# Attention visits of four key tiles where they hold a part, and norms dealt out per visit, in a fused attention and feed-forward kernel

## The chip, the cores and the metric

One core of one Trainium2 chip. The metric is the device time of one execution in microseconds (us), the median of several runs. The kernel before: 424.99 us, median of three runs from 424.94 to 425.61. The core's engines run side by side, each through its own queue in program order: TensorE (PE, matrix products), VectorE (DVE), ScalarE (ACT, functions such as exp), GpSimd (POOL), and SyncE (SP), which here only issues DMAs. Products are written to PSUM, eight banks per partition, and have to be read out of it by ACT or DVE before a bank is used again.

## The reference

Eight batches of twelve heads, 448 rows, head size 64. Each query and key row is divided by its norm, the scores are divided by tau = 0.1, softmax over the keys, times the values. The heads side by side are the 3584 x 768 input of a feed-forward layer with 2048 hidden columns:

```python
q_n = q / (norm(q, axis=-1) + 1e-06)
k_n = k / (norm(k, axis=-1) + 1e-06)
attn = softmax(q_n @ k_n.T / tau)          # per batch and head
x = (attn @ v) laid out as (3584, 768)
h = x @ moe_w_in                           # 768 -> 2048
out = maximum(0.01 * h, h) @ moe_w_out     # 2048 -> 768, float32
```

## The kernel before

**Feed-forward.** The 3584 tokens are cut into eight chunks, alternately 384 and 512 tokens wide. A chunk has 16 calls of `first` (six 128x128 matmuls each, then a leaky ReLU on ACT into `hT`) and then, for each 128 tokens, two calls of `second` (16 matmuls with 384 columns, then a copy on DVE and the DMA of the output rows by SP). A chunk can begin when the attention of its batches is in `xT`. These calls are the "feed", and together they are most of PE's work.

**Attention, its opening.** The first batches go through an opening that is laid out by hand (loops over `s`, `opened`). The change leaves this part alone, apart from the number of buffers of two pools.

**Attention, its stream.** The other 18 blocks of four heads (j = 6 to 23) are ten `GROUPS` of one or two, cut into 18 `UNITS` of two head pairs each. A unit has seven key tiles of 64 keys. One tile (`quad_tiles`) is eight small matmuls (64 rows, 32 columns, 448 queries) that run side by side in the array and fill two PSUM banks; ACT takes the exponential of both banks at once (128x896) into a `pe` buffer. The 126 tiles follow each other in `stream`, and are taken in "visits". When all tiles of a group are done, its "parts" follow, one in each of the next visits: the sums of the exponentials (`e` is None; then `group_logs` and `group_inverse` on ACT), and the values for `e` = 0 and, for groups of two, `e` = 1 (then `group_scale` on DVE, into `xT`). A part is 56 small matmuls (`group_products`) into one pair of banks. The parts of the last group come after the stream.

**A visit** (L795 to L849) issues, in this order: `normalise(s)` of a slot; `prepare()`; one tile; the part, if there is one; the other two tiles; then feed calls, with `roots(s + 1)` ahead of the last of them. Where a group of one is scaled (`alone`), `prepare()` stands behind the part.

**The norms.** A slot `s` is the queries (even) or keys (odd) of one unit. Its way: `load_qk` (two DMAs, SP) four slots ahead; `squares` (POOL); `sums` (DVE, 128x896 to 128x14); `roots` (ACT, three small operations); `normalise` (DVE, reciprocal and product, into a `qn` buffer); `transposes` (DVE, and for odd slots six DMAs on SP that bring both halves of the unit to `qkT`). `hold` is a small copy on POOL that reads `qn`, so that POOL's work behind it starts no earlier. In visit n with slot s the kernel normalises and transposes s, loads s + 4, squares s + 2, sums s + 1, and takes the roots of s + 1. `preps` gives each slot a visit of its own, three to four visits ahead of its unit.

**The planner.** `level` is the largest even share of feed per visit that the chunks' times of readiness (`at`) allow; `share` takes off the part's own cost (`side`); calls are taken from `held` while they fit. The plan is made when the program is built, so that the number of calls in each visit is fixed.

**Banks.** `banks(count)` gives the pair, or the single bank, whose last use lies furthest back, over all eight banks during the stream.

**Pools.** `qn` has three buffers, `pe` 25, `qkT` six, `ld` (raw loads) four, `hT` one.

Of the kernel before, what the change touches and what calls it, by code (L numbers as in the profile page):

```python
# [16 lines left out]
def kernel(  # L17
# [20 lines left out]
    NSLOT = B * NPAIR  # L38
# [5 lines left out]
    ATTEND = 5500  # L44
    BLOCK = 1800
    NEWQ = 2 * NQ
    PER = 3
    assert REM == 64 and D == 64

    ctx.enter_context(tc.manual_schedule())  # L50
# [2 lines left out]
    vbp = ctx.enter_context(tc.tile_pool(name="vb", bufs=3))  # L53
    sqp = ctx.enter_context(tc.tile_pool(name="sq", bufs=3))
    smp = ctx.enter_context(tc.tile_pool(name="small", bufs=3))
    qnp = ctx.enter_context(tc.tile_pool(name="qn", bufs=3))
    ttp = ctx.enter_context(tc.tile_pool(name="tt", bufs=2))
    qtp = ctx.enter_context(tc.tile_pool(name="qt", bufs=6))
    pep = ctx.enter_context(tc.tile_pool(name="pe", bufs=25))
    vqp = ctx.enter_context(tc.tile_pool(name="vq", bufs=2))  # L60
    rbp = ctx.enter_context(tc.tile_pool(name="rb", bufs=2))
    xtp = ctx.enter_context(tc.tile_pool(name="xt", bufs=2))
# [57 lines left out]
    OLD = 2 * NEWQ  # L120
# [7 lines left out]
    def load_qk(s, engs=(nc.sync, nc.sync)):  # L128
        if s >= NSLOT:
            return  # L130
        whole = ldp.tile([128, 14 * D], F32, name="qk_h")
        if s >= OLD:
            u, which = divmod(s - OLD, 2)
            for w, pair in enumerate(UNITS[u][1]):
                b, h0 = pair // NPAIR, 2 * (pair % NPAIR)
                nc.sync.dma_start(
                    out=whole[64 * w : 64 * w + 64],
                    in_=(q, k)[which][b, h0 : h0 + 2].rearrange("h (p t) d -> (h p) (t d)", t=14),
                )
            raw[s] = whole  # L140
            return
        b, h0 = s // NPAIR, 2 * (s % NPAIR)
        q_h, k_h = halves(whole)
        engs[0].dma_start(out=q_h[:, :, 0:3], in_=main(q, b, h0, 2))
        engs[1].dma_start(out=k_h, in_=main(k, b, h0, 2))
        for i, (x, eng) in enumerate(zip((q, k), engs)):
            eng.dma_start(
                out=q_h[64 * i : 64 * i + 64, :, 3],
                in_=x[b, h0 : h0 + 2, MAIN:S].rearrange("h p d -> p h d"),
            )  # L150
        raw[s] = (q_h, k_h)
# [20 lines left out]
    GROUPS = [(6,), (7, 8), (9, 10), (11,)] + [(j, j + 1) for j in range(12, 24, 2)]  # L172
# [22 lines left out]
    def squares(s, engs=(gp, gp)):  # L195
        if s >= NSLOT:
            return
        sq = sqp.tile([128, 14 * D], F32, name="sq")
        if s >= OLD:
            sqs[s] = sq  # L200
            gp.tensor_tensor(sq, raw[s], raw[s], op=ALU.mult)  # L201
            return
        sqs[s] = halves(sq)
        for x, y, eng in zip(raw[s], sqs[s], engs):
            if eng is nc.scalar:
                nc.scalar.activation(y, x, func=AF.Square)
            else:
                eng.tensor_tensor(y, x, x, op=ALU.mult)  # L208

    def sums(s, parts=(0, 1)):  # L210
        if s >= NSLOT:
            return
        if s not in ss:
            ss[s] = smp.tile([128, 14], F32, name="ss")
        if s >= OLD:
            nc.vector.tensor_reduce(  # L216
                ss[s], sqs[s].rearrange("p (t d) -> p t d", d=D), axis=AX.X, op=ALU.add
            )
            return
        for i in parts:  # L220
            o = ss[s][:, 0:8] if i == 0 else ss[s][:, 8:14]
            nc.vector.tensor_reduce(
                o.rearrange("p (h t) -> p h t", h=2), sqs[s][i], axis=AX.X, op=ALU.add
            )
# [8 lines left out]
    qn = {}  # L233

    def normalise(s):
        if s >= NSLOT:
            return
        r = smp.tile([128, 14], F32, name="r")
        nc.vector.reciprocal(r, ss[s])  # L239
        if s >= OLD:  # L240


            qn[s] = qnp.tile([128, 7, D, 2], BF16, name="qn")
            t, n = ("(m e)", "(e m)")[s % 2], 2
            nc.vector.tensor_tensor(  # L245
                qn[s].rearrange("p m d e -> p m e d"),
                raw[s].rearrange(f"p ({t[1:-1]} d) -> p m e d", e=n, d=D),
                r.rearrange(f"p {t} -> p m e", e=n).unsqueeze(3).to_broadcast([128, 7, 2, D]),
                op=ALU.mult,
            )  # L250
            return
        qn[s] = qnp.tile([128, 7, 2, D], BF16, name="qn")
        for x, lo, hi, r0 in ((raw[s][0], 0, 4, 0), (raw[s][1], 4, 7, 8)):
            nt = hi - lo
            nc.vector.tensor_tensor(  # L255
                qn[s][:, lo:hi],
                x.rearrange("p h t d -> p t h d"),
                r[:, r0 : r0 + 2 * nt].rearrange("p (h t) -> p t h", h=2)
                .unsqueeze(3).to_broadcast([128, nt, 2, D]),
                op=ALU.mult,  # L260
            )
# [129 lines left out]
    def quad_tiles(which):  # L391

        tiles = []
        for u, i in which:
            sc = banks(2)
            tiles.append(sc)
            for strip in range(4):
                x = qkT[UNITS[u][1][strip // 2]]
                c0 = S + 64 * i + 32 * (strip % 2)
                for a in range(2):  # L400
                    rows = slice(64 * a, 64 * a + 64)
                    nc.tensor.matmul(  # L402
                        out=sc[32 * strip : 32 * strip + 32, a, :S], lhsT=x[rows, c0 : c0 + 32],
                        rhs=x[rows, 0:S], start=True, stop=True,
                    )
        for (u, i), sc in zip(which, tiles):
            pq[u, i] = pe_tile()
            nc.scalar.activation(out=pq[u, i], in_=sc[:, :, :S], func=AF.Exp, scale=inv_tau)  # L408
# [169 lines left out]
    def hold(x):  # L578
        seen = smp.tile([128, 1], F32, name="seen")
        gp.tensor_copy(out=seen, in_=x)  # L580
# [183 lines left out]


    stream = [(u, i) for u in range(len(UNITS)) for i in range(7)]
    visits = [stream[n : n + PER] for n in range(0, len(stream), PER)]
    visit_of = {ui: n for n, tiles in enumerate(visits) for ui in tiles}
    parts, ready, last = {}, {}, 0
    for g, js in enumerate(GROUPS):  # L770
        last = max(last, max(visit_of[u, 6] for u, (gg, _) in enumerate(UNITS) if gg == g))
        for e in (None, 0, 1)[: 1 + len(js)]:
            last += 1
            parts[last] = (g, e)
        ready.update({j: last + 1 for j in js})
    at = {1: 0}
    for c in range(2, B):
        at[c] = ready[NQ * c + NQ - 1]
    preps, last = {}, -1
    for s in range(OLD + 3, NSLOT):  # L780
        last = max(last + 1, visit_of[(s - OLD) // 2, 0] - 4 + (s - OLD) % 2)
        preps[last] = s

    def weight(kind, cost):
        return cost * 0.7 if kind else cost
# [8 lines left out]
    held = [(False, g) for g in queue]  # L794
    fed = 0  # L795
    for n, tiles in enumerate(visits):
        s = preps.get(n, NSLOT)
        g, e = parts.get(n, (None, None))
        alone = g is not None and e is not None and len(GROUPS[g]) == 1

        def prepare():
            if s < NSLOT:
                transposes(s)
                load_qk(s + 4)
                hold(qn[s][:, 6, 0, 0:1])
                squares(s + 2)
                sums(s + 1)

        normalise(s)
        if not alone:  # L810
            prepare()
        quad_tiles(tiles[:1])
        if n == 0:
            attend(NEWQ - 1)
        if g is not None:
            po = group_products(g, e)
            if e is None:
                group_logs(g, po)
            else:
                group_scale(g, e, po)  # L820
        if alone:
            prepare()
        quad_tiles(tiles[1:])
        if g is not None and e is None:
            group_inverse(g)
        for u, i in tiles:
            if i == 6 and u and UNITS[u][0] != UNITS[u - 1][0]:
                load_vq(UNITS[u][0])
        for c in marked:
            if at[c] == n:  # L830
                held += marked[c]
        level = min(
            (sum(loads[c] for c in loads if at[c] <= x) - fed + sum(side[n : x + 1])) / (x - n + 1)
            for x in range(n, len(visits))
        )
        share = (level - side[n]) / (4 if n == len(visits) - 1 else 1)
        now, done = [], 0
        while held:
            w = weight(held[0][0], held[0][1][0])
            if now and done + w / 2 > share:  # L840
                break
            now.append(held.pop(0)[1][1])
            done += w
        fed += done
        for fn in now[:-1]:
            fn()
        roots(s + 1)
        for fn in now[-1:]:
            fn()  # L849
    g = len(GROUPS) - 1  # L850
    group_logs(g, group_products(g, None))
# [46 lines left out]
```

## Time and profile before

| | |
|---|---|
| median of three runs | 424.99 us |
| profiled execution: time, span | 425.26 us, 423.5 us |
| PE busy | 413.2 us, 98% |
| ACT busy | 267.8 us, 63% |
| DVE busy | 212.0 us, 50% |
| POOL busy | 114.7 us, 27% |
| DMA | 53.82 MB, 127 GB/s mean |
| `second`, PE matmuls (L502) | 151.4 us, 896 of 326 ns |
| `first`, PE matmuls (L474) | 151.1 us, 768 of 353 ns |
| key tiles in the stream (L402) | 38.9 us, 1008 matmuls |
| their exponentials, ACT (L408) | 109.0 us, 126 of 916 ns |
| stream of 42 visits | from 80.79 us to 348.50 us |
| PE idle in the stream, by slices | 0.37 us in 80 to 130, 0.28 in 130 to 140, none in 140 to 228, 0.28 in 228 to 244, none after |

Durations of single matmuls overlap, since several run side by side or in a pipeline; the distance from one start to the next tells what they cost. The mean granted clock of PE is 1.000 throughout. In rows of the timeline the columns are start in us, duration, engine, line, operation, output and input, size, count; a bracket gives the idle time ahead of it and what ended it.

### The profile page before, as it was taken

The numbers are of one execution on the slowest core, as the hardware profiler recorded it, in microseconds if no ns is written. First come the engines' busy times: TensorE is split into PE (matmuls) and PEld (weight loads), VectorE is DVE, ScalarE is ACT, GpSimd is POOL, SyncE is SP. The second block draws the span as 40 slices with busy tenths as digits, with TensorE's granted clock in tenths as the row PEclk, the third lists the DMA queues.
The fourth block names the chain that finished last, engine by engine and source line by source line (L and its number), as shares of the span: only waits on it lengthen the run. The fifth ranks groups of instructions, "written<-read, shape, count | busy, mean of one in ns | idle before, by whom it ended". The sixth has DMA issues, their size and how long they took to land.

```text
span 423.5 us, 11361 instructions
## 1 busy us (share of the span) xinstructions
PE 413.2 (98%) x4797; PEld 213.3 (50%) x4797; DVE 212.0 (50%) x335; ACT 267.8 (63%) x478; POOL 114.7 (27%) x150
## 2 busy tenths in 40 slices
PE   8889999999999999999999999999999999999996
PEld 3334555444455555554445555554445555654463
DVE  5877657774667645765564963465411312120021
ACT  3998885688858687758865777657774454104300
POOL 3867533533234132413231432123010000000000
PEclk9999999999999999999999999999999999999999
DMA  6999999765376953574365583543441200010021
GB/s 150 197 233 221 232 233 207 192 198 137 65 184 158 226 134 74 151 187 134 77 159 166 110 237 71 116 125 121 84 88 39 77 37 3 37 76 0 2 74 74
DMA packets 41906, 53.82 MB, mean 127 GB/s; under 512 B 12544, under 2 KB 32256, under 8 KB 41856
## 3 DMA queue, kind: packets, MB, share of 16 engines
q1 hardware_dynamic: 25536, 40.85, 34.0%
q0 software_dynamic: 15488, 11.80, 19.3%
q8 instruction: 37, 0.61, 0.6%
q10 hardware_dynamic: 832, 0.46, 0.4%
q14 instruction: 13, 0.11, 0.1%
HBM read 45.61 MB, written 11.01 MB: 134 GB/s over the span
## 4 chain that ended last, share of the span: by engine, by line
PE 84%; DVE 6%; ACT 4%; DMA 2%; issue 1%; POOL 1%; SPq 0%; POOLq 0%; DVEq 0%
PE ps L474 34%; PE ps L502 31%; PE ps L427 8%; PE ps L402 6%; DMA qk_h<-in_q_dram 2%; PE ps L571 2%; DVE qn L245 1%; ACT pe L340 1%; PE ps L351 1%; DVE ss L216 1%; DVE qn L255 1%; PE ps L331 1%; POOL sq L201 1%; ACT pe L408 1%; PE ps L269 1%
## 5 line engine op out<-in xcount | busy, mean ns | idle before, releaser
L502 PE MATMUL ps<-w_out_sb,hT 128*128 128x384 bf16 x896 | 151.4, 326 | 0.3 <-DVE xT L382 0.2
L474 PE MATMUL ps<-xT,w_in_sb 128*128 128x384 bf16 (+1 forms) x768 | 151.1, 353 | 0.0
L408 ACT ACTIVATE pe<-ps 128x896 bf16<-128x896 f32 x126 | 109.0, 916 | 42.4 <-PE ps L402 40.7
L502 PEld LDWEIGHTS <-hT 128*128 128x128 bf16 x896 | 85.4, 98 | 65.0 <-issue 10.2
L474 PEld LDWEIGHTS <-w_in_sb 128*128 128x128 bf16 x768 | 73.1, 98 | 73.6 <-issue 8.5
L480 ACT ACTIVATE hT<-ps 128x384 bf16<-128x384 f32 (+1 forms) x128 | 67.6, 547 | 59.3 <-PE ps L474 58.9
L513 DVE COPY osb<-ps 128x384 f32<-128x384 f32 (+1 forms) x56 | 30.8, 550 | 107.6 <-PE ps L502 101.9
L201 POOL TENSOR_TENSOR sq<-qk_h 128x896 f32<-128x896 f32 x36 | 60.4, 1678 | 1.6 <-DMA qk_h<-in_k_dram 1.6
L580 POOL CAST seen<-qn 128x1 f32<-128x1 bf16 x47 | 8.6, 183 | 181.3 <-DVE qn L245 168.1
L245 DVE TENSOR_TENSOR qn<-qk_h,r 128x896 bf16<-128x896 f32 x36 | 42.7, 1185 | 1.2
L239 DVE RECIPROCAL r<-ss 128x14 f32<-128x14 f32 x48 | 11.4, 237 | 59.6 <-ACT ss L231 59.6
L402 PE MATMUL ps<-qkT 64*32 64x448 bf16 x1008 | 38.9, 353 | 0.9 <-DVE xT L452 0.4
L340 ACT ACTIVATE pe<-ps 128x896 bf16<-128x896 f32 x42 | 35.8, 916 | 5.0 <-PE ps L331 3.6
L216 DVE TENSOR_REDUCE ss<-sq 128x14 f32<-128x896 f32 x36 | 37.5, 1041 | 2.6 <-POOL sq L201 2.6
L291 DVE STREAM_TRANSPOSE tt<-qn 128x448 f32<-128x448 f32 x36 | 29.6, 824 | 1.2
L452 DVE TENSOR_TENSOR xT<-ps,rb 128x448 bf16<-128x448 f32 x32 | 18.3, 613 | 21.5 <-PE ps L427 21.4
L427 PE MATMUL ps<-pe,vq 64*32 64x448 bf16 x1008 | 27.3, 349 | 0.0
L402 PEld LDWEIGHTS <-qkT 64*32 64x32 bf16 x1008 | 14.1, 91 | 21.9 <-issue 17.1
L208 POOL TENSOR_TENSOR sq<-qk_h 128x384 f32<-128x384 f32 (+1 forms) x21 | 19.5, 945 | 11.6 <-DMA qk_h<-in_k_dram 11.4
L229 ACT ACTIVATE ss<-ss,tiny 128x14 f32<-128x14 f32 x48 | 14.6, 305 | 11.6 <-DVE ss L216 9.2
L427 PEld LDWEIGHTS <-vq 64*32 64x32 bf16 x1008 | 14.7, 92 | 7.8 <-issue 0.3
L571 PE MATMUL ps<-pe 128*128 128x512 bf16 x53 | 17.0, 446 | 1.5 <-DVE pe L554 1.5
(52 smaller groups left out, 218.7 us busy)
## 6 DMA issues: line engine op xcount, KB each, us to landing
qk_h<-in_q_dram SPq DMA_DIRECT2D x36, 224.0 KB, 4.2
qk_h<-in_k_dram SPq DMA_DIRECT2D x36, 224.0 KB, 4.0
out_dram<-osb SPq DMA_DIRECT2D x20, 384.0 KB, 2.5
qkT<-tt SPq DMA_DIRECT2D x72, 56.0 KB, 2.2
qkT<-tt SPq DMA_DIRECT2D x36, 112.0 KB, 2.4
vq<-in_v_dram POOLq DMA_DIRECT2D x16, 224.0 KB, 4.9
w_in_sb<-in_moe_w_in_dram POOLq DMA_DIRECT2D x4, 768.0 KB, 9.9
w_out_sb<-in_moe_w_out_dram POOLq DMA_DIRECT2D x2, 1536.0 KB, 23.4
```

The source lines that it names most:

```text
L201: gp.tensor_tensor(sq, raw[s], raw[s], op=ALU.mult)
L216: nc.vector.tensor_reduce(ss[s], sqs[s].rearrange("p (t d) -> p t d", d=D), axis=AX.X, op=ALU.add)
L245: nc.vector.tensor_tensor(qn[s].rearrange("p m d e -> p m e d"), raw[s].rearrange(f"p ({t[1:-1]} d) -> p m e d", e=n, d=D), r.rearrange(f" ...
L291: nc.vector.transpose(out=to.rearrange(("p g (c m) -> p m g c", "p g (m c) -> p m g c")[which], m=7), in_=qn[s].bitcast(F32).rearrange("p ...
L340: nc.scalar.activation(out=dst, in_=sc[:, :, :S], func=AF.Exp, scale=inv_tau)
L402: nc.tensor.matmul(out=sc[32 * strip : 32 * strip + 32, a, :S], lhsT=x[rows, c0 : c0 + 32], rhs=x[rows, 0:S], start=True, stop=True,)
L408: nc.scalar.activation(out=pq[u, i], in_=sc[:, :, :S], func=AF.Exp, scale=inv_tau)
L427: nc.tensor.matmul(out=po[32 * strip : 32 * strip + 32, w, :S], lhsT=weights, rhs=pq[us[x if two else 0], i][rows, a, :], start=(i == 0), ...
L474: nc.tensor.matmul(out=pm[:, :n], lhsT=w_in_sb[:, kt, m * 128 : (m + 1) * 128], rhs=xT[c // 2][:, kt, c0 : c0 + n], start=(kt == 0), stop= ...
L480: nc.scalar.activation(out=hT[c][:, m, :n], in_=pm[:, :n], func=AF.Prelu, alpha=0.01)
L502: nc.tensor.matmul(out=po2[:, :HALF], lhsT=hT[c][:, m, ts * 128 : (ts + 1) * 128], rhs=w_out_sb[:, m, half * HALF : (half + 1) * HALF], st ...
L513: nc.vector.tensor_copy(out=o[:, half * HALF : half * HALF + cut], in_=po2[:, :cut])
```

## The change

Three things change together.

1. A visit that holds a part takes four tiles, any other three. Ahead of the part stand two tiles, behind it two. The parts are dealt out while the visits are cut: a group's parts are queued when its last tile has been placed, and each following visit takes one.
2. `preps` becomes a list per visit, dealt from the back: each slot as late as possible, but at least two visits ahead of its unit. A visit takes up to two slots, or one where it holds a part with `e` = 0 or 1. Squares are taken for the slots of the visit after the next, sums and roots for those of the next. `hold` stays for the last slot of a visit only. Where the part has `e` = 0 or 1, `prepare()` stands behind it.
3. The feed is dealt out per tile in place of per visit. `qn` goes from three buffers to two, `pe` from 25 to 26.

```diff
-    PER = 3
...
-    qnp = ctx.enter_context(tc.tile_pool(name="qn", bufs=3))
+    qnp = ctx.enter_context(tc.tile_pool(name="qn", bufs=2))
...
-    pep = ctx.enter_context(tc.tile_pool(name="pe", bufs=25))
+    pep = ctx.enter_context(tc.tile_pool(name="pe", bufs=26))
...
-    visits = [stream[n : n + PER] for n in range(0, len(stream), PER)]
+    visits, parts, ready, pending = [], {}, {}, []
+    while stream:
+        n = len(visits)
+        if pending:
+            parts[n] = pending.pop(0)
+            ready.update({j: n + 1 for j in GROUPS[parts[n][0]]})
+        count = 4 if n in parts else 3
+        visits.append(stream[:count])
+        stream = stream[count:]
+        for u, i in visits[-1]:
+            g = UNITS[u][0]
+            if i == 6 and (u + 1 == len(UNITS) or UNITS[u + 1][0] != g):
+                pending += [(g, e) for e in (None, 0, 1)[: 1 + len(GROUPS[g])]]
...
-    preps, last = {}, -1
-    for s in range(OLD + 3, NSLOT):
-        last = max(last + 1, visit_of[(s - OLD) // 2, 0] - 4 + (s - OLD) % 2)
-        preps[last] = s
+    preps = {}
+    for s in range(NSLOT - 1, OLD + 2, -1):
+        n = min(min(preps, default=len(visits)), visit_of[(s - OLD) // 2, 0] - 2)
+        if len(preps.get(n, [])) == (2 if parts.get(n, (0, 0))[1] is None else 1):
+            n -= 1
+        preps.setdefault(n, []).insert(0, s)
...
-        alone = g is not None and e is not None and len(GROUPS[g]) == 1
+        now, soon, later = (preps.get(n + i, []) for i in range(3))
 
         def prepare():
-            if s < NSLOT:
+            for s in now:
                 transposes(s)
                 load_qk(s + 4)
+            for s in now[-1:]:
                 hold(qn[s][:, 6, 0, 0:1])
-                squares(s + 2)
-                sums(s + 1)
-
-        normalise(s)
-        if not alone:
+            for s in later:
+                squares(s)
+            for s in soon:
+                sums(s)
+
+        for s in now:
+            normalise(s)
+        if e is None:
             prepare()
-        quad_tiles(tiles[:1])
+        ahead = 2 if g is not None else 1
+        quad_tiles(tiles[:ahead])
...
-        if alone:
+        if e is not None:
             prepare()
-        quad_tiles(tiles[1:])
+        quad_tiles(tiles[ahead:])
...
-            (sum(loads[c] for c in loads if at[c] <= x) - fed + sum(side[n : x + 1])) / (x - n + 1)
+            (sum(loads[c] for c in loads if at[c] <= x) - fed + sum(side[n : x + 1]))
+            / sum(len(w) for w in visits[n : x + 1])
...
-        share = (level - side[n]) / (4 if n == len(visits) - 1 else 1)
+        share = (level * len(tiles) - side[n]) / (4 if n == len(visits) - 1 else 1)
...
-        roots(s + 1)
-        for fn in now[-1:]:
+        for s in soon:
+            roots(s)
+        for fn in fns[-1:]:
             fn()
```

More of the change, by code (lines that the diff above doesn't have):

```diff
@@ L766 @@
     stream = [(u, i) for u in range(len(UNITS)) for i in range(7)]
-    visits = [stream[n : n + PER] for n in range(0, len(stream), PER)]
-    visit_of = {ui: n for n, tiles in enumerate(visits) for ui in tiles}
[L769 to L775, printed above, removed]
+    visits, parts, ready, pending = [], {}, {}, []
[11 more added lines that the diff above has]
+                pending += [(g, e) for e in (None, 0, 1)[: 1 + len(GROUPS[g])]]
+    assert pending == [(len(GROUPS) - 1, e) for e in (None, 0, 1)]
+    ready.update({j: len(visits) for j in GROUPS[-1]})
+    visit_of = {ui: n for n, tiles in enumerate(visits) for ui in tiles}
     at = {1: 0}
@@ L778 @@
         at[c] = ready[NQ * c + NQ - 1]
-    preps, last = {}, -1
-    for s in range(OLD + 3, NSLOT):
-        last = max(last + 1, visit_of[(s - OLD) // 2, 0] - 4 + (s - OLD) % 2)
-        preps[last] = s
+    preps = {}
[4 more added lines that the diff above has]
+        preps.setdefault(n, []).insert(0, s)
+    assert min(preps) == 0
     def weight(kind, cost):
@@ L796 @@
     for n, tiles in enumerate(visits):
-        s = preps.get(n, NSLOT)
         g, e = parts.get(n, (None, None))
-        alone = g is not None and e is not None and len(GROUPS[g]) == 1
+        now, soon, later = (preps.get(n + i, []) for i in range(3))
         def prepare():
-            if s < NSLOT:
+            for s in now:
                 transposes(s)
                 load_qk(s + 4)
+            for s in now[-1:]:
                 hold(qn[s][:, 6, 0, 0:1])
-                squares(s + 2)
-                sums(s + 1)
-        normalise(s)
-        if not alone:
+            for s in later:
[5 more added lines that the diff above has]
+        if e is None:
             prepare()
-        quad_tiles(tiles[:1])
+        ahead = 2 if g is not None else 1
+        quad_tiles(tiles[:ahead])
         if n == 0:
@@ L832 @@
         level = min(
-            (sum(loads[c] for c in loads if at[c] <= x) - fed + sum(side[n : x + 1])) / (x - n + 1)
+            (sum(loads[c] for c in loads if at[c] <= x) - fed + sum(side[n : x + 1]))
+            / sum(len(w) for w in visits[n : x + 1])
             for x in range(n, len(visits))
         )
-        share = (level - side[n]) / (4 if n == len(visits) - 1 else 1)
-        now, done = [], 0
+        share = (level * len(tiles) - side[n]) / (4 if n == len(visits) - 1 else 1)
+        fns, done = [], 0
         while held:
             w = weight(held[0][0], held[0][1][0])
-            if now and done + w / 2 > share:
+            if fns and done + w / 2 > share:
                 break
-            now.append(held.pop(0)[1][1])
+            fns.append(held.pop(0)[1][1])
             done += w
         fed += done
-        for fn in now[:-1]:
+        for fn in fns[:-1]:
             fn()
-        roots(s + 1)
-        for fn in now[-1:]:
+        for s in soon:
+            roots(s)
+        for fn in fns[-1:]:
             fn()
```

## The prediction

> **What bounds the kernel now.** I read the page's busy times and chain first, then the timeline of TensorE (PE) through the 42 visits, then ScalarE (ACT), VectorE (DVE) and the DMA issuer (SP) around single visits. "Feed" is the feed-forward groups after a visit's attention: F is a call of `first`, S of `second`. Visits count from 0.
>
> The page, busy times and chain:
>
> ```profile
> span 423.5 us, 11361 instructions
> ...
> PE 413.2 (98%) x4797; PEld 213.3 (50%) x4797; DVE 212.0 (50%) x335; ACT 267.8 (63%) x478; POOL 114.7 (27%) x150
> ...
> PE 84%; DVE 6%; ACT 4%; DMA 2%; issue 1%; POOL 1%; SPq 0%; POOLq 0%; DVEq 0%
> ```
>
> PE is the bound: any time that it waits is added to the end. Timeline of PE (start, us, line, count): visit 20, which holds a part; visit 22, which holds none; the start of visit 26:
>
> ```profile
> 204.24 0.38 PE L402 MATMUL ps<-qkT 64*32 64x448 bf16 x8
> 204.44 1.51 PE L427 MATMUL ps<-pe,vq 64*32 64x448 bf16 x56
> 205.76 0.56 PE L402 MATMUL ps<-qkT 64*32 64x448 bf16 x16
> 206.26 4.06 PE L474 MATMUL ps<-xT,w_in_sb 128*128 128x512 bf16 x18
> ...
> 216.25 0.76 PE L402 MATMUL ps<-qkT 64*32 64x448 bf16 x24
> 216.95 5.37 PE L502 MATMUL ps<-w_out_sb,hT 128*128 128x384 bf16 x32
> ...
> 237.88 0.35 PE L402 MATMUL ps<-qkT 64*32 64x448 bf16 x1
> 238.42 0.38 PE L402 MATMUL ps<-qkT 64*32 64x448 bf16 x7 [0.19 <-DVE xT L452]
> ```
>
> From start to start: attention costs 2.02 us with a part and 0.70 without; a tile is about 0.19. A feed costs its groups (S 2.60, F 1.295 with 512 columns, 0.975 with 384) plus 0.10: 32 matmuls of S take 5.30, not 5.20. Held against these, every visit from 2 on fits within 0.02 except six: 8 (0.20 over), 9 (0.52), 15 (0.35), 25 (0.19), 26 (0.53), 27 (0.13), **1.92 us of waits** in all. They lie where part visits have only one S to cover them; the last line shows why: `group_scale` stands behind the norms on DVE, and PE wants its bank.
>
> **Removed, visits.** The planner is arithmetic on counts. 25 visits hold a part, before and after; with four tiles each they take 100 of 126 tiles, so 9 plain visits are left of 17: 34 visits for 42. A plain visit costs 0.70 + 0.10 of entering and leaving, less its three tiles, which move elsewhere (0.57): 0.23. **8 x 0.23 = 1.84 saved.** Feed, parts, tiles and what follows the stream are the same work.
>
> **Removed, old waits.** After, the part visits get 5 us of feed and more, except 9, and in visits with e = 0 or 1 the scale runs ahead of transposes and sums. **1.92 saved**; what is late next is below.
>
> **Added, the bank of the second tile.** `banks` gives the pair of banks used longest ago. Before, a part visit takes the four pairs once (tile, part, tile, tile), and the feed's first group gets the first tile's. After, it is A, B, part, C, D: D takes A's pair again, and the feed begins on B's, so it waits for B's exponential. PE reaches the feed 2.02 + 0.19 = 2.21 after the visit's start. ACT in visit 20 (which follows an F):
>
> ```profile
> 204.35 0.60 ACT L480 ACTIVATE hT<-ps 128x512 bf16<-128x512 f32 x1
> 204.84 0.91 ACT L408 ACTIVATE pe<-ps 128x896 bf16<-128x896 f32 x1
> 206.21 1.73 ACT L408 ACTIVATE pe<-ps 128x896 bf16<-128x896 f32 x2 [0.46 <-PE ps L402]
> ```
>
> Roots and the last leaky ReLU hold ACT, so A's exponential starts at +0.60 (204.84 less 204.24). Two in a row take 1.72 and PE follows 0.05 later, so B's bank is free at 2.37: 0.16 late. After 384-column F it starts at +0.68 (161.70 for 161.02): 0.24 late. After an S, at +0.45 (126.62 for 126.17): 0.02. By the plan: 3, 4, 17, 18, 28, 29 follow a 512 F (0.96), 11, 23, 24 a 384 F (0.72), 12 one with no roots in its way (0.05), twelve follow an S (0.24): **1.97 added**. Bounds: nothing, if the exponentials start 0.2 earlier than in these rows; 3.0, if all 25 pay half the 0.24. D waits for A's exponential (1.51 + 0.05), and PE is there at 1.89: nothing, until A starts 0.33 later.
>
> The Trainium skill's page TensorEngine Tiling (Performance Considerations, PSUM Bottleneck) says that tiling speeds up TensorE but not the emptying of PSUM. The rows here agree: 0.19 to fill a tile, 0.81 from one exponential to the next. Taken as the bound of a whole burst it is the third rival below.
>
> **Added, two norms' roots at once.** Before visit 16, visit 15 (S, F, F) puts roots of two slots ahead of its last F's ReLU. Sums of both end 4.65 into a 6.0 us visit; ReLU 5.2, roots to 6.8 (0.8 each), last ReLU 7.3: A starts at +1.3, D waits 0.38, the feed begins at 1.3 + 1.77 = 3.07: 0.87. Visit 10 follows visit 9 (one S, 4.9 long; scale, transpose and sums end at 4.85, roots 5.65): A at +0.78, 0.34. **1.21 added.** Visits 13 and 27 also take two, but the visits before them leave room.
>
> **Added, visits 4 to 7.** The plan gives visits 5 and 6 one S each, 3.4 us, and one turn of a norm does not fit. Timeline before, visit 4 (start 108.17) into 5, with SP's issues:
>
> ```profile
> 113.08 1.04 DVE L216 TENSOR_REDUCE ss<-sq 128x14 f32<-128x896 f32 x1
> 114.16 0.31 ACT L229 ACTIVATE ss<-ss,tiny 128x14 f32<-128x14 f32 x1 [0.58 <-DVE ss L216]
> 115.09 0.24 DVE L239 RECIPROCAL r<-ss 128x14 f32<-128x14 f32 x1 [0.96 <-ACT ss L231]
> 115.36 1.17 DVE L245 TENSOR_TENSOR qn<-qk_h,r 128x896 bf16<-128x896 f32 x1
> ...
> 113.22 4.28 SPq L300 DMA_DIRECT2D qkT<-tt  x6
> 117.60 1.18 SPq L136 DMA_DIRECT2D qk_h<-in_k_dram  x2
> ```
>
> A turn is sums 1.04, roots 0.9, reciprocal and product 1.5, transpose 0.6: about 4.05. From visit 4's start after the change, the scale being 0.19 later: sums(20) end 6.15, sums(21) 10.2, roots(21) 11.05, product(21) 12.6, transpose 13.2, sums(22) 14.2. Slot 23's load stands on SP behind the six transfers of slot 19: issued 9.6 to 10.8, landed about 13.9 (3.6 in that window). Before, three visits lay between; now its squares are called one visit later: POOL 13.9 to 15.6, sums(23) 16.65, roots(23) 17.5. Behind these roots on ACT stand visit 7's exponentials: A 17.5, B done 19.2, feed 19.25. Behind sums(23) on DVE stands visit 6's S copy, which tile C's bank waits for. Unhindered, visit 7 would start at 13.15 and feed at 15.36: **3.9 added**. Lower bound: if the load is no later than the sums ahead of it, sums(23) end 15.2 and the wait is 2.4; if the turns hide, 0. Upper: 5.5, with the longest load landing (7.7, for 3.6) partly behind the chain. Unit 3's keys are needed in visit 6 at about 10 and land at 10.6 to 13; that delay lies under this one.
>
> **At nothing.** A `qn` buffer less: its readers, transpose and `hold`, stand ahead of the next writer, on DVE itself or ahead of the squares that the writer's sums need; uncovered, about 0.2 a slot (the 183 ns cast). A `pe` buffer more: the reused tile's readers are at latest the part in the same visit, done before its exponential comes up; uncovered, 1.3 (a part). Fewer holds and other turns of the DMAs: POOL is idle 73%.
>
> **Sum** against the profiled 425.26 (span 423.5 and 1.8 around it): -1.84 -1.92 +1.97 +1.21 +3.9 = +3.3, 428.6. The median is 0.27 under the profiled run: **428.3**.
>
> **Rivals.** (1) The turns of the norms hide: visits 4 to 7, 10 and 16 cost nothing, because ACT and DVE catch up within the feed. Then -1.84 -1.92 +1.97 = -1.8: **423.2**, faster. It decides at the exponentials of visit 7: started within 0.6 of its start, this holds. For it: the page has DVE at 50%. Against: visits 7 to 9 now, 4.7 long with the same turn, do wait. (2) The turn costs, but the load does not hold it (2.4) and the second tile's bank costs nothing: -3.76 +1.21 +2.4: **424.8**, no change. For it: 0.16 is near what I can read of a start. Against: B cannot be empty before 0.45 + 1.72. (3) Evacuation bounds each burst: 25 x (0.81 - 0.19) = 15.5 more, about **440**. Against: bursts of three now take 0.70 while their exponentials run to 2.9, so the banks cover it. (4) The gap in visit 7 slows the clock. The start of this trace has 22 warm-up matmuls in 7.79 us, 0.354 each for 0.216 later: 3.0 lost, so **431.3**. Against: the row PEclk is 9 throughout, though PE's longest wait here is 1.1 (at 28.6, in the opening). The Trainium skill's page TensorE: Matmul & The Clock Gate (Why this matters for your kernels) warns of idle gaps beyond about 3 us; no run so far holds such a gap.
>
> **How the numbers follow.** My sum 0.60, (1) 0.20, (2) 0.14, (3) 0.02, (4) 0.04. Within 0.2% (0.85 us) is what a measurement of this kernel cannot tell from no change. Slower: 0.66; same: 0.13, most of (2); faster: 0.21, (1) and a little of (2). The range runs from (1), 423.2, to my sum with its upper bounds (visit 7 +1.6, banks +1.0): 430.9. The forecast's own: 426.0 to 430.9.
>
> **What would show it.** Plain visits gone: 34 bursts. Feed after a part starting 2.2 to 2.45 after its burst. A PE wait of 2 to 5 us in visit 7, released by ACT's exponentials, the roots of slot 23 ahead of them, `sq` on POOL waiting for `qk_h`. If no wait over 1 us stands there, step "visits 4 to 7" is wrong; if feeds start at 2.21 after F too, the bank step is; if scale still holds PE, the removed waits are.

## The result, and the profile after

| | before | after |
|---|---|---|
| median | 425.39 us (8 runs, 424.76 to 427.4) | 428.63 us (8 runs, 427.8 to 430.67) |
| ratio | 1 | 1.0077, 95% interval 1.0056 to 1.0098 |
| profiled execution: time, span, mean clock | 425.26, 423.5, 1.000 | 429.92, 428.1, 0.996 |
| stream | 42 visits, 80.79 to 348.50 us | 34 visits, 80.99 to 353.18 us |

The kernel is 3.24 us slower, by more than 0.2%; 428.3 was forecast. Four executions of the kernel after ran at a mean granted clock of 1.000 and took 427.8 to 428.1; the other four, the profiled one among them, ran at 0.996 and took 429.2 to 430.7.

The page of the kernel after, busy times, clock in 40 slices, chain, and the squares on POOL:

```profile
span 428.1 us, 11322 instructions
...
PE 410.9 (96%) x4781; PEld 215.1 (50%) x4797; DVE 211.2 (49%) x335; ACT 267.3 (62%) x478; POOL 114.9 (27%) x146
...
PEclk9999999999998999999999999999999999999999
...
PE 72%; DMA 12%; ACT 9%; DVE 2%; SPq 1%; POOL 1%; issue 1%; POOLq 0%; DVEq 0%
...
L200 POOL TENSOR_TENSOR sq<-qk_h 128x896 f32<-128x896 f32 x36 | 60.4, 1680 | 15.2 <-DMA qk_h<-in_k_dram 15.2
```

PE's busy time reads 410.9 us for 413.2, but this isn't less work: the trace of the kernel after lacks 16 matmul records (4781 for 4797), 13 of them of `first` (755 for 768). DMA has 12% of the chain where it had 2%, and POOL's squares now wait 15.2 us for the raw loads of keys, 1.6 before. One slice of PEclk is below 9: the thirteenth, 128.4 to 139.1 us.

The timeline of the kernel after around visit 7, which starts at 123.16; visit 4 started at 108.71 and visit 6 starts at 118.46:

```profile
113.96 4.56 SPq L299 DMA_DIRECT2D qkT<-tt  x6
...
118.62 1.18 SPq L135 DMA_DIRECT2D qk_h<-in_k_dram  x2
...
123.16 0.57 PE L401 MATMUL ps<-qkT 64*32 64x448 bf16 x16
...
123.35 1.68 POOL L200 TENSOR_TENSOR sq<-qk_h 128x896 f32<-128x896 f32 x1 [4.13 <-DMA qk_h<-in_k_dram]
...
125.07 1.08 DVE L215 TENSOR_REDUCE ss<-sq 128x14 f32<-128x896 f32 x1 [1.85 <-POOL sq L200]
...
126.19 0.31 ACT L228 ACTIVATE ss<-ss,tiny 128x14 f32<-128x14 f32 x1 [2.04 <-DVE ss L215]
...
126.67 0.38 PE L401 MATMUL ps<-qkT 64*32 64x448 bf16 x8 [1.62 <-DVE osb L512]
...
126.99 1.71 ACT L407 ACTIVATE pe<-ps 128x896 bf16<-128x896 f32 x2
...
127.94 0.57 PE L401 MATMUL ps<-qkT 64*32 64x448 bf16 x8 [0.88 <-ACT pe L407]
```

Read it downwards: six key transfers hold SP, the load of slot 23 is issued behind them, POOL waits for it, DVE for POOL, ACT's roots for DVE. The exponentials of visit 7 stand behind those roots, and PE waits for a bank: for tile C for an S copy of visit 6 that stood behind the sums, for tile D for A's exponential. The feed (L501) starts at 128.74, 5.58 after the visit's start where a visit with no wait takes 2.21. In visit 6 PE also waits for unit 3's keys: its feed starts at 1.99 for 0.70. Together that is 3.37 + 1.29 = **4.66 us in visits 6 and 7**.

What follows is visible in the windows of the same execution (us; then busy time and count of PE, PEld, DVE, ACT, POOL; clock; DMA share; GB/s):

```profile
126.00:128.00 2.00, 0.45 (x16) 0.17 (x15) 1.97 (x5) 1.75 (x5) 0.85 (x1) 0.93 0.44 97
128.00:130.00 2.00, 1.77 (x13) 0.73 (x13) 1.91 (x3) 2.00 (x3) 0.18 (x1) 0.50 0.96 244
```

The clock falls to half (0.72 from 130 to 132, 1.00 after); visit 7's feed, 5.30 at full clock, takes 6.45 (128.74 to 135.19): **1.15 us**.

The second tile's bank, in the timeline of PE after: visit 19, with a part and behind an S, and visit 23, behind a 384-column F:

```profile
225.64 0.57 PE L401 MATMUL ps<-qkT 64*32 64x448 bf16 x16
...
227.87 5.36 PE L501 MATMUL ps<-w_out_sb,hT 128*128 128x384 bf16 x32
...
255.50 0.57 PE L401 MATMUL ps<-qkT 64*32 64x448 bf16 x16
...
257.94 4.22 PE L473 MATMUL ps<-xT,w_in_sb 128*128 128x384 bf16 x25 [0.17 <-ACT pe L407]
```

The first feeds 2.23 after its start, the second 2.44, its first matmul waiting for B's exponential. Read in this way for all visits of the stream, from the start of visit 2 to the first part behind the stream (254.91 us before, 259.38 after):

| | predicted | in the profiled execution |
|---|---|---|
| visits 6 and 7 | +3.9 | +4.66 |
| visit 7's feed at half clock | 0 (rival) | +1.15 |
| second tile's bank, 25 visits | +1.97 | +1.97 |
| two norms' roots: visits 16, 10 (8) | +1.21 | +0.91, +0.09 (+0.05) |
| old waits gone | -1.92 | -2.27 |
| eight visits fewer | -1.84 | -2.1, what is left |
| sum | +3.3 | +4.5 |

The last row but one is not read from a line: it is the 4.47 (259.38 less 254.91) less all other rows. The remaining 0.20 of the 4.66 between the profiled executions lies ahead of the stream (80.99 for 80.79).

The old waits are 2.27, and not 1.92, because the prediction's reading passed over visits 13 and 29 of the kernel before. PE and DVE in visit 13 before:

```profile
163.04 2.12 PE L474 MATMUL ps<-xT,w_in_sb 128*128 128x384 bf16 x12
165.17 2.76 PE L502 MATMUL ps<-w_out_sb,hT 128*128 128x384 bf16 x16
167.86 0.38 PE L402 MATMUL ps<-qkT 64*32 64x448 bf16 x8
...
163.54 1.04 DVE L216 TENSOR_REDUCE ss<-sq 128x14 f32<-128x896 f32 x1
164.50 1.14 DVE L452 TENSOR_TENSOR xT<-ps,rb 128x448 bf16<-128x448 f32 x2
```

Two F and an S take 4.82 us (163.04 to 167.86, the start of visit 14) where the costs in the prediction give 4.65: 0.17 over. No bracket shows it, since the matmuls overlap; the starts do. The third group of the feed comes round to the part's bank, which the scale on DVE, behind the sums, empties only from 164.50 on. Visit 29 has 5 F in 5.15 for 4.975, 0.18 over. In both runs below with the scale ahead of the norms these two are gone. In the kernel after no wait of this kind is left.

### The profile page after: what moved, and what is told of

Its sections match the earlier page's. It is cut to its first block, busy times and chain, and to the rows that moved or that the text cites. A ratio compares the mean times of both kernels' runs of the same rounds, so it can differ in the third digit from the quotient of the medians.

```text
span 428.1 us, 11322 instructions
## 1 busy us (share of the span) xinstructions
PE 410.9 (96%) x4781; PEld 215.1 (50%) x4797; DVE 211.2 (49%) x335; ACT 267.3 (62%) x478; POOL 114.9 (27%) x146
## 4 chain that ended last, share of the span: by engine, by line
PE 72%; DMA 12%; ACT 9%; DVE 2%; SPq 1%; POOL 1%; issue 1%; POOLq 0%; DVEq 0%
PE ps L501 34%; PE ps L473 28%; DMA qk_h<-in_k_dram 6%; PE ps L426 5%; DMA w_out_sb<-in_moe_w_out_dram 5%; ACT pe L407 4%; PE ps L401 4%; ACT hT L479 2%; DMA qk_h<-in_q_dram 2%; ACT ss L230 1%; ACT ss L228 1%; ACT ss L229 1%; SPq L299 1%; PE ps L350 1%; POOL v_rem L169 0%
## 5 line engine op out<-in xcount | busy, mean ns | idle before, releaser
L501 PE MATMUL ps<-w_out_sb,hT 128*128 128x384 bf16 x896 | 151.9, 328 | 1.6 <-DMA w_out_sb<-in_moe_w_out_dram 1.2
L473 PE MATMUL ps<-xT,w_in_sb 128*128 128x384 bf16 (+1 forms) x755 | 149.0, 352 | 2.3 <-ACT pe L407 0.9
L407 ACT ACTIVATE pe<-ps 128x896 bf16<-128x896 f32 x126 | 107.4, 921 | 36.7 <-PE ps L401 36.3
L501 PEld LDWEIGHTS <-hT 128*128 128x128 bf16 x896 | 86.3, 98 | 66.0 <-issue 9.6
L473 PEld LDWEIGHTS <-w_in_sb 128*128 128x128 bf16 x768 | 74.1, 98 | 74.1 <-issue 7.4
L200 POOL TENSOR_TENSOR sq<-qk_h 128x896 f32<-128x896 f32 x36 | 60.4, 1680 | 15.2 <-DMA qk_h<-in_k_dram 15.2
L244 DVE TENSOR_TENSOR qn<-qk_h,r 128x896 bf16<-128x896 f32 x36 | 43.6, 1210 | 1.4
L401 PE MATMUL ps<-qkT 64*32 64x448 bf16 x1008 | 37.2, 354 | 3.6 <-DVE osb L512 1.6
L339 ACT ACTIVATE pe<-ps 128x896 bf16<-128x896 f32 x42 | 35.8, 916 | 5.9 <-PE ps L330 4.5
L290 DVE STREAM_TRANSPOSE tt<-qn 128x448 f32<-128x448 f32 x36 | 28.7, 813 | 0.6
L401 PEld LDWEIGHTS <-qkT 64*32 64x32 bf16 x1008 | 12.0, 90 | 21.7 <-issue 16.3
L570 PE MATMUL ps<-pe 128*128 128x512 bf16 x50 | 15.1, 420 | 1.9 <-DVE pe L553 1.5
```

The lines of the kernel that those rows point to most:

```text
L244: nc.vector.tensor_tensor(qn[s].rearrange("p m d e -> p m e d"), raw[s].rearrange(f"p ({t[1:-1]} d) -> p m e d", e=n, d=D), r.rearrange(f" ...
L290: nc.vector.transpose(out=to.rearrange(("p g (c m) -> p m g c", "p g (m c) -> p m g c")[which], m=7), in_=qn[s].bitcast(F32).rearrange("p ...
L339: nc.scalar.activation(out=dst, in_=sc[:, :, :S], func=AF.Exp, scale=inv_tau)
L401: nc.tensor.matmul(out=sc[32 * strip : 32 * strip + 32, a, :S], lhsT=x[rows, c0 : c0 + 32], rhs=x[rows, 0:S], start=True, stop=True,)
L473: nc.tensor.matmul(out=pm[:, :n], lhsT=w_in_sb[:, kt, m * 128 : (m + 1) * 128], rhs=xT[c // 2][:, kt, c0 : c0 + n], start=(kt == 0), stop= ...
L501: nc.tensor.matmul(out=po2[:, :HALF], lhsT=hT[c][:, m, ts * 128 : (ts + 1) * 128], rhs=w_out_sb[:, m, half * HALF : (half + 1) * HALF], st ...
```

## The experiments

My theory: visits 6 and 7 lose because the norms' turns meet short visits there, with the load of slot 23 on top; the old waits came from the scale behind the norms; the second tile's bank waits where the roots are late. Rivals: the load alone, the split of the feed alone, the pools, or the bank as the main cost.

**Load ahead of the transposes.** In the kernel after, slot s + 4 is loaded before the six key transfers of slot s instead of behind them.

```diff
             for s in now:
-                transposes(s)
                 load_qk(s + 4)
+                transposes(s)
```

> The changed kernel, with load_qk(s + 4) ahead of transposes(s), so that SP issues a slot's load before the six transfers of an odd slot. Theory (slot 23's load stands behind six transfers and lands too late for visit 7): the load lands about 8 us earlier, sums(23) follow sums(22) at once, and the feed of visit 7 starts about 18.1 us after visit 4's start instead of 20.0 (128.74 less 108.71): 1.9 less. The gap is then shorter, and the clock stays at 1.000 in most executions: about 425.9 us. Rival (the turn of norms on DVE and ACT alone holds visit 7; the load would be in time): no change, 428.6 us.

Measured: 426.92 us (426.68 to 427.35), ratio to before 1.0041 (1.0028 to 1.0054). Its timeline, with visit 4 from 108.40:

```profile
110.15 1.11 SPq L135 DMA_DIRECT2D qk_h<-in_k_dram  x2
...
122.17 2.04 DVE L215 TENSOR_REDUCE ss<-sq 128x14 f32<-128x896 f32 x2
...
126.79 5.36 PE L501 MATMUL ps<-w_out_sb,hT 128*128 128x384 bf16 x32 [0.42 <-ACT pe L407]
```

Counted from visit 4's start, the load goes out 8.2 us earlier (1.75 for 9.91), the sums of slots 22 and 23 follow each other without a wait, and visit 7 feeds 18.39 after visit 4's start, for 20.03: 1.64 us is the load's share. The other 3.03 over the unhindered 15.36 stays: it is the turns themselves. No execution had a clock below 0.998.

**Feed dealt out per visit again**, in the kernel after:

```diff
-            / sum(len(w) for w in visits[n : x + 1])
+            / (x - n + 1)
...
-        share = (level * len(tiles) - side[n]) / (4 if n == len(visits) - 1 else 1)
+        share = (level - side[n]) / (4 if n == len(visits) - 1 else 1)
```

> The changed kernel, with the feed dealt out per visit as before instead of per tile; by the planner's arithmetic visits 5 and 6 then have two S each and visits 7 and 8 one. Theory (visits of 3.4 us are too short for a turn of norms of about 4 us): the waits of visits 6 and 7 (1.29 + 3.37 us, and 1.15 at a lowered clock) go; 1.1 in visit 8, 0.2 in 9, 0.3 in 10 take their place: about 424.9 us, clock 1.000. Rival (what costs are the four tiles and the banks, in all part visits alike): the time stays near 428 us.

Measured: 425.65 us (424.77 to 427.34), ratio 1.0014 (0.9999 to 1.003). PE in visits 5 and 6 (the S after each) and in visit 8, from 133.19:

```profile
116.97 5.37 PE L501 MATMUL ps<-w_out_sb,hT 128*128 128x384 bf16 x32
...
122.96 5.37 PE L501 MATMUL ps<-w_out_sb,hT 128*128 128x384 bf16 x32
...
133.19 0.57 PE L401 MATMUL ps<-qkT 64*32 64x448 bf16 x16
...
136.57 2.76 PE L501 MATMUL ps<-w_out_sb,hT 128*128 128x384 bf16 x16 [0.42 <-ACT pe L407]
```

Visits 5 and 6 have two S each (32 matmuls), and the wait of visits 6 and 7 is gone. Part of it comes back in the visits that now have one S: 1.17 in visit 8 (feed at 3.38 for 2.21), 0.78 in 9. The bank's waits are those of the kernel after. So the large loss comes from the meeting of short visits with the norms, not the bank.

**The scale ahead of the norms, in the kernel before.** Every visit with values, not only those of groups of one, puts `prepare()` behind the part. It ran twice, on different chips.

```diff
-        alone = g is not None and e is not None and len(GROUPS[g]) == 1
+        alone = g is not None and e is not None
```

> The kernel before, with prepare() behind the part in every visit whose part has e = 0 or 1, not only where a group of one is scaled: group_scale is then ahead of transposes and sums on DVE, one part of the change alone. Theory (the 1.92 us of waits in visits 8, 9, 15, 25, 26, 27 are the scale's, which holds a pair of banks): 0.4 us or less is left of them, about 423.5 us. Rival (in visits with one S of feed DVE is the bound, and the wait only moves from the scale to the norms): 425 us, no change.

> The kernel before with the scale ahead of prepare(), beside the one above on the same chip, to see which is the faster. Theory: 42 visits without the scale's waits take 423.3 us in executions at a clock of 1.000, the same as 34 visits with the bank waits or 0.5 less. Rival: 34 visits are faster by 1.3 or more.

Measured: 424.26 us (422.53 to 425.34), ratio 0.9977 (0.996 to 0.9993); and 423.59 us (422.67 to 425.76), ratio 0.9959 (0.9942 to 0.9977). The end of visit 25 and the start of visit 26 on PE, in the first of the two:

```profile
235.84 2.76 PE L502 MATMUL ps<-w_out_sb,hT 128*128 128x384 bf16 x16
238.53 0.38 PE L402 MATMUL ps<-qkT 64*32 64x448 bf16 x8
238.73 1.51 PE L427 MATMUL ps<-pe,vq 64*32 64x448 bf16 x56
```

Before, the next visit started with one matmul and a wait `<-DVE xT`; here its first tile runs at once. Of the 2.27 us about 0.6 is left (0.25 each in visits 9 and 26, 0.05 in 8 and 25). So the old waits were the scale behind the norms, and this one line, without the larger visits, is faster than both kernels.

**The pools alone**, in the kernel before:

```diff
-    qnp = ctx.enter_context(tc.tile_pool(name="qn", bufs=3))
+    qnp = ctx.enter_context(tc.tile_pool(name="qn", bufs=2))
...
-    pep = ctx.enter_context(tc.tile_pool(name="pe", bufs=25))
+    pep = ctx.enter_context(tc.tile_pool(name="pe", bufs=26))
```

> The kernel before, with two qn buffers for three and 26 pe buffers for 25, nothing else. Theory (the readers of a qn buffer are done before its next writer): no change, 425.0 to 425.4 us. Rival (normalise waits for the hold or the transposes of the slot two earlier): up to 0.2 us in each of 33 slots of the stream, part of it hidden, 426 us or more.

Measured: 426.32 us (423.92 to 427.69), ratio 1.0018 (0.9995 to 1.0042). The interval holds 1, and by itself it would allow a loss of some 1.8 us. The trace shows no new wait: from visit 2 to the first part behind the stream it takes 254.81 us, the kernel before 254.91.

**The roots ahead of the last two feed calls**, in the kernel after:

```diff
-        for fn in fns[:-1]:
+        for fn in fns[:-2]:
             fn()
         for s in soon:
             roots(s)
-        for fn in fns[-1:]:
+        for fn in fns[-2:]:
             fn()
```

> The changed kernel, with the roots of the next visit's slots issued ahead of the last two feed calls instead of the last one. Theory (the feed after a part waits for the bank of the second tile, whose exponential is late where roots and the last ReLU hold ACT): the wait of visit 16 falls from 0.91 to 0.2 us, those of 11, 23 and 24 (after 384-column F) from 0.23 to about 0.05, those after 512-column F stay at 0.16, because there the last ReLU itself ends at +0.6; visits 6 and 7, with one S, stay as they are: 1.3 less, 427.3 us. Rival (the 0.16 and 0.23 are PE's own change of tile shape, with four tiles): no change in any of these visits, 428.6 us.

Measured: 428.03 us (427.78 to 428.67), ratio 1.0069 (1.0046 to 1.0093): no gain that can be told. The bank's wait fell in visits 11, 23 and 24 from 0.23 to 0.05, as the theory has it. But visit 5 now waits 0.88, and visit 16, which has roots of two slots ahead of it, 1.28 for 0.91. ACT and PE in its start, at 194.72:

```profile
194.68 0.31 ACT L228 ACTIVATE ss<-ss,tiny 128x14 f32<-128x14 f32 x1
...
195.48 1.06 ACT L479 ACTIVATE hT<-ps 128x512 bf16<-128x512 f32 x2
...
196.11 1.51 PE L426 MATMUL ps<-pe,ones 64*32 64x448 bf16 x55 [0.60 <-ACT hT L479]
```

Two leaky ReLUs instead of one now stand behind the roots, and the part waits for their bank. I had not counted that.

**The roots last of all**, in the kernel after and in the kernel before (there `now` for `fns`, `s + 1` for `s`): this delays every exponential that follows an F, so that the bank of the second tile, if it is what counts, must cost more in the one than in the other.

```diff
-        for fn in fns[:-1]:
+        for fn in fns:
             fn()
         for s in soon:
             roots(s)
-        for fn in fns[-1:]:
-            fn()
```

> The changed kernel, with the roots of the next visit's slots behind all feed calls, so that they stand between the last ReLU and the first tile's exponential on ACT. Theory (bank of the second tile): the feed after a part begins 0.9 after it could, instead of 0.16 to 0.23, in the ten visits that follow an F with roots, and 1.7 in visit 16: about 7 us more, 435 us. Rival (ACT's lateness is spread over the feed and reaches PE nowhere): 428.6 us.

> The kernel before with the same edit. Its part visits use each pair of banks once, and the feed begins on the first tile's, whose exponential now ends 0.25 us after PE could start. Theory (the bank decides): 0.25 in each of some 12 part visits that follow an F, about 3 us more, 428 us, less than half of what the changed kernel pays. Rival (the order on ACT costs both kernels alike): 7 us more here too, 432 us.

Measured: after 436.24 us (435.27 to 439.26), ratio 1.0273 (1.0233 to 1.0313); before 431.15 us (430.8 to 431.47), ratio 1.0142 (1.0107 to 1.0176). Visit 3 in both, first of the kernel after, then of the one before:

```profile
99.28 0.57 PE L401 MATMUL ps<-qkT 64*32 64x448 bf16 x16
...
100.67 1.70 ACT L407 ACTIVATE pe<-ps 128x896 bf16<-128x896 f32 x2
...
102.42 0.81 PE L473 MATMUL ps<-xT,w_in_sb 128*128 128x512 bf16 x2 [0.42 <-ACT pe L407]
```

```profile
100.58 0.38 PE L402 MATMUL ps<-qkT 64*32 64x448 bf16 x8
...
101.97 0.90 ACT L408 ACTIVATE pe<-ps 128x896 bf16<-128x896 f32 x1
...
102.92 0.38 PE L474 MATMUL ps<-xT,w_in_sb 128*128 128x512 bf16 x1 [0.25 <-ACT pe L408]
```

A's exponential starts 1.39 into the visit in both. The kernel of four tiles feeds at 3.14, 0.93 late, since it waits for two exponentials; the kernel of three at 2.34, 0.32 late, since it waits for one. That is the bank as predicted (0.83 behind 384 columns, against 0.21). The totals don't tell the two apart: the kernel before was expected at 428 and took 3 more, since the later roots delay normalise, and with it the scale behind it on DVE, and in six visits the feed takes 0.25 to 0.90 longer, waiting `<-DVE xT`. It is the start of the feed in each visit that shows the bank.

**The three mends together**: load first, feed per visit, roots ahead of the last two calls, in the kernel after (edits as above).

> The changed kernel with the loads ahead of the transposes, the feed dealt out per visit, and the roots ahead of the last two feed calls. Theory: the feed per visit takes the waits of visits 6 and 7 (425.3 us in executions at a clock of 1.000), the earlier roots 1.3 of the bank waits, the earlier loads nothing more: 424.0 us at a clock of 1.000, faster than the kernel before. Rival (with one S in visits 7, 8 and 9 the norms hold those visits whatever comes before): 425.3 us or more.

Measured: 424.95 us (423.89 to 426.93), ratio 0.9999 (0.9979 to 1.002). Visits 8 (1.17), 5 (0.88), 11, 23 and 24 (0.05) wait as with the single edits; visits 9 and 16 fell further, to 0.31 and 0.16. The loss is gone, but the gain that was expected (424.0 at a clock of 1.000) isn't there.

**Two slots only where there is no part**: as built, the limit lets a visit with the sums take two slots and a visit without a part only one, since `parts.get(n, (0, 0))[1]` is 0 there and not `None`; the description of the change ahead of the prediction has this the wrong way round for visits without a part. This kernel turns it over, with load first and feed per visit, and ran on one chip with the second run of the scale ahead of the norms.

```diff
-        if len(preps.get(n, [])) == (2 if parts.get(n, (0, 0))[1] is None else 1):
+        if len(preps.get(n, [])) == (1 if n in parts else 2):
```

> The changed kernel with the loads ahead of the transposes, the feed per visit, and two slots of norms allowed in visits without a part instead of those with the sums: slots 21 and 22 in visit 6, 31 and 32 in 15, 43 and 44 in 26. Theory (once the norms hide, what four tiles save in changes of tile shape, 1.84, they pay back at the second tile's bank, about 2): visits 5 to 8 wait 0.3 or less each, 9 and 10 0.3, 16 0.16, the others as in the changed kernel, 2.9 in all; 423.8 us in executions at a clock of 1.000. Rival (the bank waits are small change, and without the norms' waits 34 visits beat 42): 422 us.

Measured: 424.67 us (424.22 to 427.71), ratio 0.9991 (0.9971 to 1.0011), against 423.59 for the scale ahead of the norms beside it. From visit 2 to the first part behind the stream the profiled executions take 254.85 and 253.19 us, of which 4.37 and 0.61 are waits. (2.9 was expected for the first: visits 6, 8 and 9 wait 0.85, 0.75 and 0.34.) Without the waits they would be 250.48 and 252.58: eight visits fewer save 2.1 us, and the bank (about 2) and what is left of visits 6, 8 and 9 take more than that back.

## Why the prediction was right

**What bounds.** PE bounds, and every wait of it goes to the end: the waits that the trace shows, with the removed visits, give 4.5 of the 4.66 between the two profiled executions.

**Removed, visits.** 34 bursts, as the count had it, and 2.1 us by what is left of the profiled pair and by the last experiment, for 1.84: 0.26 a visit for 0.23. The same comes out of the other profiles: from visit 2 to the first part behind the stream, less the waits and the 1.15 at the lowered clock, the five profiles with 42 visits have 252.5 to 252.6 us left, and the seven with 34 have 250.5. The price came from differences of starts, each read within 0.02.

**Removed, old waits.** The cause was right and the size too small: "every visit from 2 on fits within 0.02 except six" doesn't hold for visits 13 and 29, so that 2.27 us went for 1.92. Shown: with the scale ahead of the norms alone, 0.6 of the 2.27 is left.

**Added, the bank of the second tile.** 0.16 behind 512 columns, 0.23 and 0.24 behind 384, 0.05 in visit 12, 0.02 behind an S: each by its own visit, and the sum of 1.97. The cause is shown by the three runs that move the roots: it went down to 0.05 where they came earlier and up to 0.93 where they came later. The exponential is what empties the bank too late, but it holds only the second tile's bank and not the whole burst, so that rival (3) with 440 falls. The Trainium skill's page TensorEngine Tiling (Array Packing) says (Performance Considerations, PSUM Bottleneck) that tiling makes TensorE faster and leaves the emptying of PSUM as it was. The waits of 0.16 to 0.24 agree with it.

**Added, two norms' roots at once.** 0.91 in visit 16 for 0.87; 0.09 in visit 10 for 0.34, since A's exponential started 0.55 into the visit, not 0.78.

**Added, visits 4 to 7.** The place, the chain and the releasers were right; the size was 4.66 for 3.9. Step by step, from visit 4's start: load issued at 9.9 (predicted 9.6), squares at 14.64 (13.9), A's exponential at 18.28 (17.5), feed at 20.03 (19.25). So the term that was too small is the load's: the transfers ahead of it took 4.56 us, not 4.28, and from issue to squares it took 4.73, not 4.3. Everything behind it kept its distance. That "unit 3's keys ... lies under this one" held: visit 6 waits 1.29, and the feed of visit 7 is set by the other chain all the same. The load's own share was 1.64 (worked out as 3.9 less the lower bound of 2.4: 1.5), so that rival (2) falls; the feed per tile was needed for the rest, as the run with the feed per visit shows, so rival (1), in which the turns hide, falls too: it wanted visit 7's exponentials within 0.6 of its start, and they start at 3.83 (126.99 less 123.16).

**The clock.** I gave rival (4) 0.04 and wrote that the row of PEclk spoke against it. In the profiled execution it happened, at 1.15 us and not 3.0. That visit 7's gap also lowered the clock of the three others at 0.996 isn't shown: the kernel before, which has no such gap, ran at 0.994 to 0.996 in 16 of the 72 executions beside the experiments, and in the two other profiles at 0.996 (feed per visit, and the first of the scale ahead of the norms) the fall lies in the opening.

The four executions at a clock of 1.000 have no profile, so what their visits 6 and 7 lost isn't known. The run with the load first, all at 0.998 and more, is 0.9 below them (426.92 for 427.85), less than the 1.64 that the two traces show; but the start of visit 2 alone differs by 0.8 between profiles at such a clock (92.82 to 93.59). Two of these, with the roots earlier and with the roots last, still have the feed per tile, and their visits 5 to 7 wait 4.4 and 4.7 us. So the loss doesn't need the lowered clock; its size in those four stays open.

**At nothing.** The pools showed no wait, and the stream took as long with them as without.

That the median came within 0.3 us is partly luck. Errors cancel: old waits, visits saved and visit 10 together came out 0.8 better than forecast, visits 6 and 7 0.8 worse. What is left over in the profiled stretch, 4.47 for 3.3, is the clock's 1.15; and the median, 428.63, lies between the executions at a clock of 1.000 (427.85 in the median, 0.45 below the forecast) and those at 0.996.

## What to carry to other kernels

Fewer and larger bursts save what it costs to enter and leave them (0.26 us each here), but a burst that comes round to a bank it has used itself waits for the engine that empties it: count banks and exponentials per burst before enlarging it, and see what stands ahead of the first one on that engine. Work that used to have a visit of its own needs a visit as long as its chain; where work is dealt out per visit and its cover per tile, the short visits meet the long chains. And look for the cheap half of a change: the order of two steps on DVE alone gave a ratio to before of 0.9959 (0.9942 to 0.9977), and no version of the whole change came below 0.9991 (0.9971 to 1.0011).

## What was not expected of the hardware

The granted clock fell to 0.50 with no wait of PE above 1.62 us. From 125.05 to 128.74 PE waited 1.62, 0.88 and 0.23 us, with sixteen small matmuls between; it was busy 0.45 of the 2 us up to 128, and the clock was 0.93 in these, 0.50 in the next 2 us and 0.72 in the two after that. The same dip stands in the opening of the profiled execution with the feed per visit (clock 0.93, 0.50, 0.72 from 28 to 34 us, with PE busy 0.65 of the first two), ahead of the stream.

Thin work alone doesn't decide it. The kernel before was busy 0.69 of the same 2 us of its opening (28 to 30), and its clock stayed at 1.00. With the roots earlier, PE waited 1.26, 0.88 and 0.42 us in visit 7 and was busy 0.74 and 0.72 in two windows of 2 us in a row (124 to 128), at a clock of 1.00; with the load ahead of the transposes it was 1.12 and 1.57, at 1.00 too.

The Trainium skill's page TensorE: Matmul & The Clock Gate (Why this matters for your kernels) warns of idle gaps beyond about 3 us. Here several shorter ones in a row went with the dip. How thin the work has to be, and why the same program shows the dip in one execution and not in the next, isn't settled.
